# One more first layer by seven products, w1 asked for ahead of w2, and the striking out queued behind the list

## The chip, the core and the metric

The kernel runs on one core of a Trainium2 chip. The core has several engines with a queue of instructions each: TensorE (PE, matrix products; its loads of stationary weights are listed apart, as PEld), VectorE (DVE), ScalarE (ACT), GpSimd (POOL, which here mostly issues gathers and scatters) and SyncE (SP, which issues the plain transfers). A queue is worked off in order; between queues, semaphores make one engine wait for another. The metric is the time of one execution on the device, in microseconds (us). The kernel before takes 395.65 us (median of 3 runs, 395.48 to 396.61).

## The reference

The task joins an attention block to a layer of experts. The attention is a recurrence over 768 steps, for 4 batches of 8 heads of 48 elements:

```python
for t in range(S):
    cur = np.einsum('bhd,bhe->bhde', u[None] * kt, vt)
    y[:, :, t] = np.einsum('bhd,bhde->bhe', rt, state + cur)
    state = w[None, :, :, None] * state + np.einsum('bhd,bhe->bhde', kt, vt)
```

Its output is 3072 rows (tokens) of D = 384. Each row is then given to one of E = 8 experts, and each expert takes exactly 384 rows: all 3072 x 8 scores are sorted downwards, and a score's row goes to the score's expert unless the row has one already or the expert is full. Each expert then does two dense layers on its rows, without bias:

```python
h = np.maximum(x[mask] @ w1[e], 0.0)      # w1[e]: 384 x 1024
out[mask] = h @ w2[e]                     # w2[e]: 1024 x 384
```

Everything is 32-bit floating point.

## The kernel before

**Stages.** The attention fills the first 150 us or so, in an order written out by hand. The remaining 245 us belong to the experts: seven of them in turn with all their 384 rows (numbered 1 to 7 in the order in which the assignment fills them), and one, the "star", in two pieces: 256 rows already within the attention, the last 128 at the very end. In this second part the program text gives the work, and a planner at compile time orders the instructions of each engine by its own cost estimates; on the chip each queue then keeps that order.

**An expert.** `run` (from L1764) goes through the experts. For each it does a first layer (`hid`, 1024 x 384 hidden values, kept transposed) and a second layer. A product of 128 x 128 weights with 128 x 384 data takes TensorE two records in the trace, because the numbers have 32 bits.

- The plain first layer, `hidden` (L1613; its products are line L1621), does 24 products of 128 x 384.
- The other, `hidden_by_seven` (L1562), splits w1, x and the result into 2 x 2 blocks and gets the four result blocks from seven products of sums of blocks in place of eight, a form of Strassen's method. `weight_sums` (L1538) makes four sums of weight blocks (`first_T`, 128 x 512, line L1545), `row_sums` (L1549) five sums of blocks of rows (`first_S`, 128 x 192), both on VectorE. `FIRST` (L1551) names the products P1 to P7, `FIRST_ORDER` their order. In this case the third 128 of D has no partner and is simply added in, so that the layer takes 44 products of 128 x 192, that is 88 records. ScalarE copies P1, P5 and P6 aside, and VectorE adds other products to them (`kept_P`, L1590, 128 x 384). The products appear as `h_ps`, `hb_ps` and `hc_ps` (L1598).
- The second layer of most experts is `seven` for 256 of the rows (L1695, `pa_ps`, `pb_ps`, `pc_ps`; weight and row sums `T`, `S` on L1670) and a plain `result` for the last 128 rows (L1753, `o_ps`, 16 records). For experts 6 and 7 it is `fifteen`, fifteen products of sums for all 384 rows (L1726); its ten weight sums `W` and eleven sums of hidden blocks `H` come from L1670 too.

Which experts take `hidden_by_seven` is written in one line:

```python
FIRST_BY_SEVEN = 3, 6, 7
```

When expert n is in its second layer, `progress` (in `run`) makes the next expert's `weight_sums` and `turn` makes its turned rows `xT` and `row_sums`, if n + 1 is in that list.

**The assignment.** Beside the products, `walk` (class Assignment, L733) finds out which rows the next expert gets. One search is `likely_steps` (L1021). In each of three rounds VectorE marks the scores above 16 candidate thresholds (`ind`), TensorE counts the marks (L945), VectorE prepares the counts (`own`, `cnt`, `wide`), TensorE adds them over all partitions (L956), and VectorE takes the next finer thresholds from the result (`most`, `full`, `dg`, `cand`; in the last round `full_e`, `dge`, ... `acc`). Then TensorE makes running totals (`st_ps`, L1076 and L1077; for the last expert L1379 and L1380), from which VectorE gets `place`. `tokens` (L1392) makes the list of the expert's rows of it: VectorE `lo`, `hi`, `row`, `oh`, `vals`, TensorE `some_ps` (L1409), VectorE `some`, `part`, TensorE `list_ps` (L1427), VectorE `mine`, `tok` (L1433). `leave` (L1003) strikes the taken rows out of the scores: `fe`, `dead` and a masked write to the scores (L1012), then two small updates. The generator `later` (L1918) hands `run` these steps, a few during each expert; the search that runs during expert n's first layer ends ahead of the fetch for expert n + 1.

**Fetching.** `fetch` (L1521) gathers the rows (`xg`, L1515, GpSimd) and calls `load_weights` (L1497), which makes the expert's `number` on VectorE, reads it into a register of SyncE, and asks for both weights, 1536 KB each, in two transfers from SyncE's queue:

```python
for t, src in ((w2, moe_w2), (w1, moe_w1)):
    nc.sync.dma_start(t, src[ds(E - e, 1)].rearrange("o (c p) f -> p (o c) f", p=128))
```

The tiles w1, w2, xg and xT exist twice, for even and odd experts, so a transfer for expert n waits until expert n - 2 has done with that tile, and what stands behind it in SyncE's queue waits as well.

Of the kernel before, what the change touches and what calls it, by code (L numbers as in the profile page):

```python
# [16 lines left out]
ALU = mybir.AluOpType  # L17
# [715 lines left out]
class Assignment:  # L733
# [689 lines left out]
    def numbers(self, part, NC, tok):  # L1423

        nc, pool, Q = self.nc, self.pool, 128 // self.LO
        list_ps = self.ps.tile([128, NC, Q], F32, name="list_ps", tag="few")
        nc.tensor.matmul(list_ps.rearrange("p c q -> p (c q)"), self.alike, part, start=True, stop=True)  # L1427
        mine = pool.tile([128, NC, Q], F32, name="mine")
        nc.vector.scalar_tensor_tensor(out=mine, in0=list_ps, scalar=float(64 * self.NT),
                                       in1=self.quarter.unsqueeze(1).to_broadcast([128, NC, Q]),  # L1430
                                       op0=ALU.add, op1=ALU.mult)
        with nc.allow_low_precision(reason="whole numbers"):
            nc.vector.tensor_reduce(out=tok, in_=mine, axis=AX.X, op=ALU.add)  # L1433

    def in_order(self, tok):

# [13 lines left out]
def rwkv5_eagle_then_base_layer_balanced(  # L1450
# [34 lines left out]
    class Experts:  # L1485
# [13 lines left out]
        def load_weights(self, n, fmax):  # L1499
            number = walk.outs.tile([1, 1], I32, name="number")  # L1500
            nc.vector.tensor_scalar(out=number, in0=fmax[0:1, :], scalar1=1.0, scalar2=float(E),
                                    op0=ALU.max, op1=ALU.min)
            pool = self.turns[n % 2]
            w1, w2 = pool.tile([128, KD, F], F32, name="w1"), pool.tile([128, KF, DX], F32, name="w2")
            e = nc.values_load(number[0:1, 0:1], engines=(mybir.EngineType.SP,), min_val=1, max_val=E,
                               skip_runtime_bounds_check_because="held between 1 and E")
            for t, src in ((w2, moe_w2), (w1, moe_w1)):
                nc.sync.dma_start(t, src[ds(E - e, 1)].rearrange("o (c p) f -> p (o c) f", p=128))
            return w1, w2

# [248 lines left out]
            nc.scalar.copy(o_sb, o_ps)  # L1759
            self.scatter(o_sb, tok[:, c:c + 1], to)  # L1760

        FIRST_BY_SEVEN = 3, 6, 7

        def run(self, ahead, later, rows, pulls={}, xT=None):  # L1764
            xT, lead = xT or self.turn(ahead), True
# [97 lines left out]
    with ExitStack() as whole:  # L1863
# [68 lines left out]
        def later():  # L1932
            yield from search
            walk.bound(ident)
            now = second
            for n in range(2, 5):
                walk.book(now, first=True)
                yield x.fetch(n, now["fmax"], walk.tokens(now["place"]))
                walk.leave(now)
                yield  # L1940
                now = walk.new_outs()
                yield from walk.likely_steps(**now)
            was = now
            walk.book(was)
            walk.leave(was)
            for n in range(5, E):
                rest = n == E - 1
                yield
                if rest:
                    yield  # L1950
                    now = walk.remainder()
                else:
                    now = walk.new_outs()
                    yield from walk.likely_steps(**now)
                walk.book(now, surely=rest)
                walk.choose(was, now)
                yield x.fetch(n, was["fmax"], walk.tokens(was["place"]))
                if not rest:
                    walk.leave(now)
                was = now  # L1960
            yield
            yield
            tc.mark_branch_hint_location("whole")
            have["ok"] = walk.found()
            yield x.fetch(E, walk.star, walk.tokens(walk.star_place, 1))
# [50 lines left out]
```

## Time and profile before

The profiled execution is one run on the chip with the hardware profiler.

| | before |
|---|---|
| median of 3 runs | 395.65 us (395.48 to 396.61) |
| the profiled execution's own time | 395.83 us |
| its span, from first to last record | 394.1 us |
| granted TensorE clock over the span | 0.998 |
| TensorE busy | 381.2 us, 97% of the span |
| VectorE busy | 281.3 us, 71% |
| ScalarE busy | 169.1 us, 43% |
| GpSimd busy | 141.0 us, 36% |
| weight transfers (w1, w2) | 18 of 1536 KB, median 9.0 us from issue to landing |

Busy time by stretch of the experts' part (the stretches begin and end with a layer):

| stretch, us | what TensorE works on | TensorE busy | VectorE busy |
|---|---|---|---|
| 252.3 to 269.3 | expert 4, first layer (plain) | 16.81 | 14.40 |
| 269.3 to 285.4 | expert 4, second layer | 15.79 | 8.70 |
| 285.4 to 302.15 | expert 5, first layer (plain) | 16.75 | 12.84 |
| 302.15 to 317.8 | expert 5, second layer | | 12.90 |
| 317.8 to 332.7 | expert 6, first layer (by seven) | | 10.83 |
| 332.7 to 347.4 | expert 6, second layer (fifteen) | | 14.34 |
| 347.4 to 362.8 | expert 7, first layer (by seven) | 14.81 | 8.83 |

How to read it: busy times are sums over one engine's instructions; engines work beside each other. A line of the timeline gives the start, the duration, the engine, the line of the kernel, the operation, output and inputs with their shapes, and how many instructions of the kind stand in a row; a bracket gives the idle time of the engine ahead of it, and whose work ended that. Idle time of an engine matters only if others wait for it. Ends of products are modelled, so pitches are taken from start to start.

### The profile page before, as it was taken

The page shows a single profiled execution, that of the slowest core. Times are in us where ns is not written, and L with a number is a line of the kernel's source. Part 1 is how long each engine was busy: PE and PEld are TensorE (multiplying, and loading weights), DVE is VectorE, ACT ScalarE, POOL GpSimd, SP SyncE. Part 2 cuts the span into 40 slices and gives each one's busy share as a digit, 9 for nine tenths or more (in the row PEclk, how much of TensorE's full clock was granted, in tenths as well). Part 3 has the DMA queues.
Part 4 walks back from the last instruction along what each step waited for, and adds up shares of the span by engine and source line. Part 5 has one row for each costly group of instructions (what it writes and reads, how often), then busy time and mean ns, then how long its engine had stood idle before and what let it go on. Part 6 is the DMA issues. An engine that isn't in the chain of part 4 may idle for free. (4 is left out here: it accounts for less than half of the span.)

```text
span 394.1 us, 9090 instructions
## 1 busy us (share of the span) xinstructions
PE 381.2 (97%) x3393; PEld 309.5 (79%) x3393; DVE 281.3 (71%) x959; ACT 169.1 (43%) x452; POOL 141.0 (36%) x173
## 2 busy tenths in 40 slices
PE   8999999999999999999999999999999999999993
PEld 7778888888887766677568799558756889989991
DVE  6855777576786778986859949978378976994530
ACT  4997878788883411222222242121222233234130
POOL 7888877656742013032121121202303202070020
PEclk9999999999999999999999999999999999999999
DMA  9999999987592155461470470109209265181010
GB/s 120 160 182 172 197 196 182 171 175 146 113 360 78 58 188 231 145 237 42 119 280 22 132 290 20 41 2 339 83 20 318 97 214 194 38 331 33 2 62 27
DMA packets 95332, 57.30 MB, mean 145 GB/s; under 512 B 77232, under 2 KB 89520, under 8 KB 95280
## 3 DMA queue, kind: packets, MB, share of 16 engines
q1 hardware_dynamic: 91936, 47.21, 47.7%
q0 software_dynamic: 3104, 9.44, 6.9%
q8 instruction: 28, 0.46, 0.5%
q14 instruction: 24, 0.20, 0.2%
q10 hardware_dynamic: 240, 0.00, 0.0%
HBM read 47.20 MB, written 9.44 MB: 144 GB/s over the span
## 5 line engine op out<-in xcount | busy, mean ns | idle before, releaser
L1621 PE MATMUL h_ps<-xT,w 128*128 128x384 f32 (+1 forms) x264 | 72.6, 427 | 0.0
L495 ACT ACTIVATE AT<-ident,dd 128x128 f32<-128x128 f32 x192 | 59.7, 394 | 1.2 <-DVE dd L448 1.1
L1621 PEld LDWEIGHTS h_ps<-xT,w 128*128 128x128 f32 x264 | 42.0, 191 | 19.6 <-issue 2.2
L1515 POOL DMA_INDIRECT xg<-x_rows,tok x22 | 22.2, 1008 | 92.3 <-PE h_ps L1621 23.7
L1747 POOL DMA_INDIRECT out_dram<-o_all,to x16 | 20.8, 1301 | 85.8 <-DVE o_all L1735 22.2
L508 DVE COPY_PREDICATED AT<-mask,g_ps 128x512 f32<-128x512 uint8 x48 | 32.7, 733 | 13.1 <-PE g_ps L504 11.5
L1624 ACT ACTIVATE hid<-h_ps 128x384 f32<-128x384 f32 (+1 forms) x40 | 17.9, 449 | 54.2 <-PE h_ps L1621 50.9
L1753 PE MATMUL o_ps<-w,hid 128*128 128x384 f32 x96 | 32.5, 490 | 0.0
L504 PE MATMUL g_ps<-rT,kT 48*128 48x128 f32 x384 | 27.9, 284 | 1.0 <-ACT x L561 0.6
L436 POOL TENSOR_TENSOR kss<-krs,wk 128x384 f32<-128x384 f32 x24 | 24.3, 1014 | 8.0 <-DVE krs L340 5.2
L504 PEld LDWEIGHTS g_ps<-rT,kT 48*128 48x128 f32 x384 | 23.4, 187 | 4.3 <-ACT AT L495 0.9
L1753 PEld LDWEIGHTS o_ps<-w,hid 128*128 128x128 f32 x96 | 17.7, 190 | 10.6 <-issue 0.5
L542 PE MATMUL y_ps<-AT,vts 128*64 128x128 f32 x384 | 25.7, 276 | 0.0
L443 POOL TENSOR_TENSOR rk<-rk,u_bc 128x384 f32<-128x384 f32 x24 | 24.2, 1009 | 1.9
L442 POOL TENSOR_TENSOR rk<-krs 128x384 f32<-128x384 f32 x24 | 24.5, 1019 | 0.2 <-DVE chunk L650 0.2
L542 PEld LDWEIGHTS y_ps<-AT,vts 128*64 128x64 f32 x384 | 20.6, 137 | 0.9 <-issue 0.3
L477 DVE TENSOR_TENSOR rT<-rT_ps,WR 112x512 f32<-112x512 f32 x23 | 15.8, 686 | 5.1 <-PE rT_ps L458 5.1
L561 ACT COPY x<-y_ps 128x512 f32<-128x512 f32 x24 | 14.1, 588 | 8.6 <-PE y_ps L542 8.6
L448 DVE TENSOR_REDUCE dd<-rk 128x8 f32<-128x384 f32 x24 | 13.1, 546 | 6.3 <-POOL rk L443 6.3
L458 PE MATMUL rT_ps<-ident,krs 128*112 128x128 f32 x96 | 15.5, 283 | 0.5 <-ACT krs L344 0.4
L1695 PE MATMUL pa_ps<-T,S 128*128 128x192 f32 x80 | 15.8, 331 | 0.0
L1726 PE MATMUL p_ps<-W,H 128*128 128x128 f32 x128 | 15.8, 275 | 0.0
(340 smaller groups left out, 831.3 us busy)
## 6 DMA issues: line engine op xcount, KB each, us to landing
w<-in_moe_w_dram SPq DMA_DIRECT2D x18, 1536.0 KB, 9.0
krs<-in_k_dram SPq DMA_DIRECT2D x24, 192.0 KB, 4.5
krs<-in_r_dram SPq DMA_DIRECT2D x24, 192.0 KB, 5.0
vts<-in_v_dram SPq DMA_DIRECT2D x24, 192.0 KB, 5.0
x_rows<-xr SPq DMA_DIRECT2D x24, 192.0 KB, 3.3
xg<-x_rows,tok POOLq DMA_INDIRECT x22, 4.0
out_dram<-o_all,to POOLq DMA_INDIRECT x16, 2.7
out_dram<-o_sb,to POOLq DMA_INDIRECT x5, 2.6
```

What stands on the lines that cost most here:

```text
L436: self.nc.gpsimd.tensor_mul(self.kss[:, n % self.NS].rearrange("p (g h) d -> p g h d", g=2)[:, :, :, 0:D], src, self.wk.rearrange("p (g h) ...
L442: nc.gpsimd.tensor_mul(rk, self.krs[:, n % self.NK, 1, 0:H, 0:D], self.krs[:, n % self.NK, 0, 0:H, 0:D])
L443: nc.gpsimd.tensor_mul(rk, rk, self.u_bc)
L495: nc.scalar.mul(AT[:, z, a, :], self.ident, dd[:, h:h + 1])
L504: nc.tensor.matmul(g_ps[:, z, a, :], kT[rows, a, :], rT[rows, a, :], start=True, stop=True)
L508: nc.vector.copy_predicated(out=AT[:, z], mask=self.mask.unsqueeze(1).to_broadcast([128, HP, T]), data=g_ps[:, z])
L542: nc.tensor.matmul(yv[q * PD:(q + 1) * PD, o // 2, o % 2, :], lhsT, rhs, start=(o // 2, q) not in seen, stop=stop, skip_group_check=True)
L1515: nc.gpsimd.indirect_dma_start(out=xg[:, c, :], out_offset=None, in_=x_dram[0:within, :], in_offset=bass.IndirectOffsetOnAxis(ap=tok[:, c: ...
L1621: nc.tensor.matmul(h_ps[j][:, at], w1[:, f, ts(j, 128)], xT[:, f, at], start=(f == 0), stop=(f == KD - 1))
L1624: nc.scalar.activation(hid[:, j, 0:m], h_ps[j][:, 0:m], AF.Relu)
L1747: nc.gpsimd.indirect_dma_start(out=to, out_offset=bass.IndirectOffsetOnAxis(ap=tok, axis=0), in_=o_sb, in_offset=None)
L1753: nc.tensor.matmul(o_ps, hid[:, j, ts(c, 128)], w2[:, j, :], start=(j == 0), stop=(j == KF - 1))
```

## The change

Three things are changed. Expert 5 joins the list of experts whose first layer goes by seven products of sums; so its four weight sums and five row sums are made during expert 4's second layer. Of every expert's weights, w1 is now asked for first and w2 second (this holds for all nine pairs, also in the part of the program that only runs if the search fails). And in the last part of `later`, for experts 5 and 6 in the loop, the strike-out `walk.leave(now)` is tied, by `tc.issue_after`, to the last instruction of the list (`tok`, remembered as `walk.listed`): it is placed in the queue behind that instruction, and so is the next search, which reads the scores it writes.

```diff
-            nc.vector.tensor_reduce(out=tok, in_=mine, axis=AX.X, op=ALU.add)
+            self.listed = nc.vector.tensor_reduce(out=tok, in_=mine, axis=AX.X, op=ALU.add)
...
-            for t, src in ((w2, moe_w2), (w1, moe_w1)):
+            for t, src in ((w1, moe_w1), (w2, moe_w2)):
                 nc.sync.dma_start(t, src[ds(E - e, 1)].rearrange("o (c p) f -> p (o c) f", p=128))
...
-        FIRST_BY_SEVEN = 3, 6, 7
+        FIRST_BY_SEVEN = 3, 5, 6, 7
...
                 if not rest:
-                    walk.leave(now)
+                    with tc.issue_after(walk.listed.ins):
+                        walk.leave(now)
                 was = now
```

The order of the instructions in the queues follows from these through the planner. In the compiled program TensorE's queue is the same up to the second layer of expert 2. There the search's counts stand one round earlier. In expert 3's first layer the list's two products stand half a wide product later; in expert 4's first layer `some_ps` stands two wide products earlier. Expert 5's first layer begins, with every number a count of 128 x 192 products (two records each): L956, 5, L945, 5, L956, 5, L945, 5, L956, 7, L1076, 13, L1409, 3, L1427. In expert 7's first layer the star's `list_ps` stands one such product earlier. The rest of TensorE's order is the same. On VectorE, the strike-out stands behind `tok` in the searches of experts 4 and 5's layers, and the additions of `kept_P` in expert 5's first layer stand between `cnt` and `wide` (rounds two and three), ahead of `full_e`, and ahead of `some`.

## The prediction

> **What bounds the kernel now.** I read the page's busy shares first, then its clock row, then the TensorE timeline of the experts' part (150 us to the end), then the VectorE timeline beside it, the weight transfers last.
>
> ```profile
> PE 381.2 (97%) x3393; PEld 309.5 (79%) x3393; DVE 281.3 (71%) x959; ACT 169.1 (43%) x452; POOL 141.0 (36%) x173
> PEclk9999999999999999999999999999999999999999
> w<-in_moe_w_dram SPq DMA_DIRECT2D x18, 1536.0 KB, 9.0
> ```
>
> TensorE (PE) is busy for 381.2 of 394.1 us at an even clock (0.998 over the run), so whatever takes time off PE's own row shortens the run, and a cut elsewhere counts only where PE stood still for it. The timeline (columns: start, us, engine, line, operation, out and in, shape, count; in brackets the idle time before it) shows expert 5's first layer, which the change rewrites:
>
> ```profile
> 280.23 5.32 PE L1753 MATMUL o_ps<-w,hid 128*128 128x384 f32 x16
> 285.39 0.22 PE L956 MATMUL counts<-wide,ones_h 128*128 128x128 f16 x1
> 285.45 2.15 PE L1621 MATMUL h_ps<-xT,w 128*128 128x384 f32 x6
> 287.44 0.25 PE L945 MATMUL counts<-prop,ind 128*128 128x64 bf16 x3
> 287.52 1.54 PE L1621 MATMUL h_ps<-xT,w 128*128 128x384 f32 x4
> 288.90 0.22 PE L956 MATMUL counts<-wide,ones_h 128*128 128x128 f16 x1
> ...
> 302.15 1.46 PE L1695 MATMUL pa_ps<-w,hid 128*128 128x192 f32 x8
> 303.45 1.46 PE L1695 MATMUL pc_ps<-w,hid 128*128 128x192 f32 x8
> ```
>
> The reader is to see three things. There is no bracket: PE doesn't wait here. One product is two records, and records follow at a pitch: 285.45 to 302.15 for 48 wide ones, and (303.45 - 302.15) / 8 = 0.1625 us for one 192 columns wide. And the search ahead of expert 6's fetch is woven in: counting matmuls (L956, L945) stand between the products at places written into PE's queue, and VectorE must answer each before PE reaches the next. VectorE's side of one such exchange:
>
> ```profile
> 285.65 0.29 DVE L1044 TENSOR_REDUCE most<-counts 128x16 f32<-128x128 f32 x1 [4.26 <-PE counts L956]
> 286.67 0.55 DVE L933 TENSOR_TENSOR ind<-m,cand 128x384 bf16<-128x384 f32 x1
> 203.51 1.30 DVE L1545 TENSOR_TENSOR first_T<-w 128x512 f32<-128x512 f32 x2 [4.67 <-DMA w<-in_moe_w_dram]
> 329.11 0.69 DVE L1545 TENSOR_TENSOR first_T<-w 128x512 f32<-128x512 f32 x1 [3.19 <-DMA w<-in_moe_w_dram]
> ```
>
> `ind` ends at 287.22 and L945 starts at 287.44, so PE arrives about 0.2 us after it could. The other two lines are the waits for w1, which lands second of its pair.
>
> **The change part by part.** The sum is made against the profiled execution, 395.83 us (span 394.1 and 1.73 around it); it stands 0.18 over the median 395.65, to which I apply the difference.
>
> *Expert 5's products.* It removes 24 products of 384 columns (48 records) and adds 44 of 192 (88 records). The last sixteen wide records of the second layer before it (312.60 to 317.76, expert 5's own) give 5.16 / 16 = 0.3225; another stretch of 22 (197.22 to 204.40) gives 0.3264. At their middle 0.3244: 48 x 0.3244 = 15.57 us against 88 x 0.1625 = 14.30 us. That is -1.27 (with the two pitches -1.2 to -1.4), all of it on PE's row. Rows that exist already agree: experts 3 and 6 by seven products take 220.85 to 235.83 and 317.81 to 332.69, some 14.9 with their interleaved counts, against 16.70 here.
>
> [...]
>
> *The search inside it.* In the changed queue only five narrow products (10 records, 1.63 us) stand between L956 and L945, five between L945 and the next L956, seven between the last L956 and the totals (L1076). Against that:
> - L956 to L945 needs 285.39 to 287.22 plus a hand-over of about 0.07: 1.9 us. Covered are 1.63 + 0.06 for the count itself, so PE waits about 0.2, twice: +0.4.
> - L945 to L956 needs 287.44 to 288.59 (`wide` begins 288.30 and lasts 0.29) and about 0.07, 1.22. The additions of kept products (`kept_P`, 0.55 each, 0.47 in a row) come into VectorE's queue between `cnt` and `wide` in rounds two and three; 1.69 against 1.63 + 0.06: 0.
> - Last L956 (292.40) to L1076 needs `acc` (294.20 + 0.24 = 294.44), 2.1 us, and the addition of P6 before `full_e`, 0.47: 2.57 against 7 x 0.325 = 2.28: +0.25.
> Together +0.65. Lower bound 0: nothing of it shows, since VectorE is busy for only 12.84 of the 16.75 us here. Upper bound: all five additions land in exchanges in full, 5 x 0.55 = 2.75, with the 0.4: +3.15. I take the middle reading because the additions whose place I see lie in covered stretches except one.
>
> *Sums of weights and rows for expert 5.* Four `first_T` (pitch 0.60) and five `first_S` (0.27), 3.75 us of VectorE in expert 4's second layer, where it is busy 8.70 of 15.79 us: hidden. Without that cover they would cost up to 3.75. The first products need raw weights, only the third kind (P5) needs S1 and T1.
>
> *Striking out behind the list.* `fe`, `dead`, the masked write of LG (0.21 + 0.34 + 0.41) leave the place ahead of the list and stand behind `tok`; behind them now wait SEVEN_LATE's first sum S1 and the next search. In expert 5's second layer P5, which needs S1, starts nine narrow products (2.93 us) behind the list's last matmul (L1427). `tok` ends 0.61 behind that (300.53 + 0.17 - 300.09); the strike-out 0.96, the sums S3 and S1 1.30 (0.65 each, 295.06's row) and some 0.18 of hand-over and small operations make 3.05: 0.12 late. Before, P2 and P5 there lay 0.23 over their pitch in the timeline; I take -0.1 (-0.23 to +0.12). In expert 4's first layer the list's first product (L1409) comes two wide products (4 x 0.3244 = 1.30) earlier:
>
> ```profile
> 269.17 0.31 PE L1409 MATMUL some_ps<-vals,row 128*128 128x48 f16 x6 [0.19 <-DVE vals L933]
> 350.51 0.18 PE L1427 MATMUL list_ps<-part,alike 128*128 128x4 f16 x1 [0.59 <-DVE part L1418]
> ```
>
> It waited 0.19 for `vals` before. Ahead of `vals` VectorE is spared `dead`, LG and the next search's `m`, `prop` and `ind` (pitches there 0.25, 0.33, 0.26, 0.27, 0.47: 1.58); as some filled the 0.36 between `upto` and `after`, which depends on it, I count 1.2 and a wait of 0.29: +0.1 (-0.19, the wait goes, to +0.3, if 1.0 is spared). Expert 3's list comes half a product later: -0.05.
>
> *Star's list.* The second line is PE's longest wait for VectorE in this part. Its L1427 now comes one product (0.325) earlier in PE's queue, while VectorE's `part` is moved by -0.1 to +0.3: +0.2, bounds -0.59 (the wait goes) and +0.62 (0.325 + 0.3).
>
> *w1 ahead of w2.* No instruction is added on SP, POOL or the transfer queue: nine pairs change order, each register load as before. SP waits for the place of the first it asks for. For expert 5 the pair was asked at 265.23 and 265.86, w2 came in 266.3 to 271.5 and w1 270.9 to 275.4: one behind the other, so w1 comes about 5 us earlier and w2 as much later. That ends the waits of 4.67 and 3.19 on VectorE, but PE was busy beside both: 0. Late next is w2: expert 6's ten `W` sums begin when w2 lands, and before waited for it 1.47 us at 302.76; they have till the second layer's products of them. In expert 2's second layer, where VectorE no longer stands waiting for w1, the search's counts move one round earlier in PE's queue: 0, bounds -0.3 to +0.3 (half a round's slack of the kind above).
>
> The trace's first-of-pair transfers land 6.8 us or more after their issue. [...]
>
> Sum: -1.27 + 0.65 - 0.1 + 0.1 - 0.05 + 0.2 + 0 + 0 = -0.47. 395.65 - 0.47 = 395.2 us; profiled 395.4, span 393.6.
>
> **The rivals.** *Clean gain.* The exchanges are covered after all (VectorE's own idle times in that stretch, 0.36 to 0.56 ahead of `own` and `full_e` in its timeline, speak for it) and star's wait shrinks by half: -1.27 - 0.3 - 0.1 = -1.7, or -1.27 alone: 393.9 to 394.4. Against it: 10 narrow records are shorter than the 1.9 us chain.
>
> *VectorE takes over (the other side).* In expert 5's first layer the five additions of kept products fall into the search's exchanges, in front of `wide`, `full_e` and `some`, so that PE stands at L956, L1076 and L1409. Price: 5 x 0.55 + 0.4 - 1.27 = +1.9: 397.5. It decides from waits of 1.27 on, and shows as slower from 2.46 on, which is four of the five additions in full and the 0.4. For it: additions wait for PE's own products, thus for the engine that waits for them. Against: expert 3's layer by seven carries the same five beside three interleaved counts in 14.98 us, and there
>
> ```profile
> 232.68 0.55 DVE L1590 TENSOR_TENSOR kept_P<-kept_P,hc_ps 128x384 f32<-128x384 f32 x1 [3.99 <-PE hc_ps L1598]
> ```
>
> VectorE had been idle 3.99 us.
>
> *w2 now too late.* Expert 6's w2 lands where w1 did (302.2 becomes 306.3), so its ten `W` sums (0.60 pitch, 6.0 us) start 4 us later, and the search and list for 7 or a product by `fifteen` wait: one and a half sums' pitch, +0.9, on the forecast: 396.1, within 0.3%.
>
> **How the numbers follow.** 0.3% is 1.19 us, about what a measurement of this kernel can tell from no change: faster is below 394.46, slower above 396.84. Forecast 0.42 (own range 394.5 to 395.9), clean gain 0.30, VectorE takes over 0.18, w2 too late 0.10, of which 0.02 slower. So faster 0.30, within 0.50, slower 0.20. The forecast's lower bounds reach the clean gain's, its upper ones (3.15, 0.62, 0.3) VectorE's; 393.8 to 397.3 leaves out about 0.2, a tenth on each side.
>
> **What would show it.** Right: 88 records at 0.1625 where the 48 stood; 0.1 to 0.3 us in brackets before two L945 and the L1076 of that layer; no `first_T` line with a DMA behind it; about 0.5 before star's L1427. Clean gain: no bracket there. VectorE: brackets of 0.5 or more naming `wide`, `acc` or `vals`. w2: a bracket before a product by `fifteen` naming `W`. The prediction is wrong if the part up to 204 us differs, or if the narrow pitch exceeds 0.17 there.

## The result, and the profile after

The changed kernel takes 397.25 us (median of 10 runs, 396.84 to 397.54), the kernel before 395.66 (10 runs). The ratio is 1.0035, 95% interval 1.0026 to 1.0045: slower by about 1.4 us (0.0035 of 395.66), just past the 0.3% that the forecast counted as the bound to no change. The forecast was 0.47 us faster. The profiled execution's span is 395.5 us against 394.1.

The page of the changed kernel, its busy shares, clock, the group of gathers (out<-in, count, busy us, mean ns of one, idle before) and the weight transfers:

```profile
PE 380.4 (96%) x3433; PEld 314.2 (79%) x3433; DVE 288.2 (73%) x974; ACT 172.3 (44%) x458; POOL 148.3 (37%) x173
PEclk9999999999999999999999999999999999999997
L1515 POOL DMA_INDIRECT xg<-x_rows,tok x22 | 29.4, 1335 | 89.8 <-PE h_ps L1621 39.7
w<-in_moe_w_dram SPq DMA_DIRECT2D x18, 1536.0 KB, 7.0
```

TensorE is busy 0.8 us less (380.4 for 381.2), in a span that is 1.4 us longer: it stands still for some 2.2 us more. The granted clock was 1.00 in both kernels up to 390 us, behind the last product, so the clock is no part of it. The third line is the odd one. The same 22 gathers took 22.2 us of GpSimd before (mean 1008 ns), and take 29.4 now.

Where the time goes is read from the TensorE timeline, by the start of each stage in both kernels:

| stretch | after less before, us |
|---|---|
| up to expert 3's list | 0.02 |
| expert 3's list, in its first layer | +0.26 |
| expert 4's list | +0.17 |
| turning of expert 5's rows, in expert 4's second layer | +0.44 |
| start of expert 5's first layer to product P2 of its second layer | -0.83 |
| from there to the turn | -0.20 |
| turning of expert 6's rows, in expert 5's second layer | +1.48 |
| the star's list | +0.08 |
| sum | +1.42 |

The two turns, from TensorE's timeline of the changed kernel (brackets: idle time and what ended it):

```profile
268.31 0.31 PE L1409 MATMUL some_ps<-vals,row 128*128 128x48 f16 x6 [0.34 <-DVE vals L933]
...
279.78 0.52 PE L1530 MATMUL xT_ps<-ident,xg 128*128 128x128 f32 x3 [0.63 <-DMA xg<-x_rows,tok]
...
286.33 0.87 PE L1598 MATMUL h_ps<-xT,w 128*128 128x192 f32 x4
287.03 1.14 PE L1598 MATMUL hc_ps<-xT,w 128*128 128x192 f32 x6
288.16 0.26 PE L945 MATMUL counts<-prop,ind 128*128 128x64 bf16 x3
...
311.30 0.52 PE L1530 MATMUL xT_ps<-ident,xg 128*128 128x128 f32 x3 [0.78 <-DVE o_all L1685]
...
312.60 0.52 PE L1530 MATMUL xT_ps<-ident,xg 128*128 128x128 f32 x3 [0.45 <-DMA xg<-x_rows,tok]
...
351.69 0.18 PE L1427 MATMUL list_ps<-part,alike 128*128 128x4 f16 x1 [0.76 <-DVE part L1418]
```

The same transposes in the kernel before:

```profile
278.90 0.52 PE L1530 MATMUL xT_ps<-ident,xg 128*128 128x128 f32 x3 [0.31 <-ACT xT L1531]
...
310.18 0.82 PE L1530 MATMUL xT_ps<-ident,xg 128*128 128x128 f32 x6
...
311.24 0.55 PE L1530 MATMUL xT_ps<-ident,xg 128*128 128x128 f32 x3
```

All three L1530 lines of the changed kernel are transposes of gathered rows (`xg`), and two name the gather's transfer. They start 0.14 us after their rows landed (279.64 and 312.46 by the trace's landing signals). The wait that is put down to `o_all` is the second block of the same rows; `o_all` ended at 311.28, but these rows landed at 311.16, again 0.14 ahead of the transposes. So the rows come late, though both lists are ready in time. GpSimd's timeline of the changed kernel shows why:

```profile
270.57 0.99 POOL L1515 DMA_INDIRECT xg<-x_rows,tok  x1 [16.03 <-PE h_ps L1621]
271.86 4.40 POOL L1515 DMA_INDIRECT xg<-x_rows,tok  x1 [0.30 <-issue]
276.57 0.95 POOL L1515 DMA_INDIRECT xg<-x_rows,tok  x1 [0.30 <-issue]
...
303.14 0.99 POOL L1515 DMA_INDIRECT xg<-x_rows,tok  x1 [14.95 <-PE h_ps L1598]
304.44 4.67 POOL L1515 DMA_INDIRECT xg<-x_rows,tok  x1 [0.30 <-issue]
309.41 0.95 POOL L1515 DMA_INDIRECT xg<-x_rows,tok  x1 [0.30 <-issue]
```

The same six gathers in the kernel before:

```profile
272.82 0.99 POOL L1515 DMA_INDIRECT xg<-x_rows,tok  x1 [18.56 <-PE pc_ps L1695]
274.12 1.30 POOL L1515 DMA_INDIRECT xg<-x_rows,tok  x1 [0.30 <-issue]
275.72 0.98 POOL L1515 DMA_INDIRECT xg<-x_rows,tok  x1 [0.30 <-issue]
...
301.47 0.99 POOL L1515 DMA_INDIRECT xg<-x_rows,tok  x1 [14.15 <-issue]
302.77 0.96 POOL L1515 DMA_INDIRECT xg<-x_rows,tok  x1 [0.30 <-issue]
304.04 1.00 POOL L1515 DMA_INDIRECT xg<-x_rows,tok  x1 [0.31 <-issue]
```

In the changed kernel the second of each three gathers stands for 4.40 and 4.67 us; most others take 0.95 to 0.99 us. And this is what VectorE does in the second case:

```profile
303.38 1.29 DVE L1670 TENSOR_TENSOR S<-hid 128x512 f32<-128x512 f32 x2
304.58 0.68 DVE L1545 TENSOR_TENSOR first_T<-w 128x512 f32<-128x512 f32 x1
305.19 0.68 DVE L1670 TENSOR_TENSOR S<-S,hid 128x512 f32<-128x512 f32 x1
305.79 0.68 DVE L1545 TENSOR_TENSOR first_T<-w,first_T 128x512 f32<-128x512 f32 x1
306.39 0.68 DVE L1670 TENSOR_TENSOR S<-hid,S 128x512 f32<-128x512 f32 x1
307.00 0.68 DVE L1545 TENSOR_TENSOR first_T<-w 128x512 f32<-128x512 f32 x1
307.60 0.68 DVE L1545 TENSOR_TENSOR first_T<-w,first_T 128x512 f32<-128x512 f32 x1
308.20 0.34 DVE L1685 TENSOR_TENSOR o_all<-kept_P,pc_ps 128x192 f32<-128x192 f32 x1
```

Eight sums of 128 x 512 without a pause, each with two inputs in SBUF, and then `o_all`, which takes one input from PSUM (the `_ps` tiles, where TensorE's products land; the other tiles here lie in SBUF). The gather ends at 309.11, which is 0.91 us after `o_all` begins: almost exactly the length of an undisturbed gather. At expert 5 it is the same: `o_all` begins at 275.35, the gather ends at 276.26. The gather looks as if it had got through only when the run ended.

A run as long is new at this place. Before, w1 for the next expert landed second, so `first_T` stood behind other work (308.01 for expert 6) and VectorE's queue behind the list was held up by the wait for w2. Now w1 is there when the list is, and hidden sums and weight sums follow each other without a break just when the gathers are issued. But a run by itself isn't enough. The kernel before has a shorter one at the same place, which ends with an `o_all` at 305.94:

```profile
302.76 0.73 DVE L1670 TENSOR_TENSOR W<-w 128x512 f32<-128x512 f32 x1 [1.47 <-DMA w<-in_moe_w_dram]
303.52 0.69 DVE L1670 TENSOR_TENSOR W<-W,w 128x512 f32<-128x512 f32 x1
304.13 0.68 DVE L1670 TENSOR_TENSOR S<-hid 128x512 f32<-128x512 f32 x1
304.74 0.68 DVE L1670 TENSOR_TENSOR W<-W,w 128x512 f32<-128x512 f32 x1
305.34 0.68 DVE L1670 TENSOR_TENSOR S<-S,hid 128x512 f32<-128x512 f32 x1
```

Two gathers were issued into it, at 302.77 and 304.04, and got through in 0.96 and 1.00 us.

### The profile page after: what moved, and what is told of

Its sections match the earlier page's. It is cut to its first block, busy times and chain, and to the rows that moved or that the text cites. A ratio compares the mean times of both kernels' runs of the same rounds, so it can differ in the third digit from the quotient of the medians.

```text
span 395.5 us, 9206 instructions
## 1 busy us (share of the span) xinstructions
PE 380.4 (96%) x3433; PEld 314.2 (79%) x3433; DVE 288.2 (73%) x974; ACT 172.3 (44%) x458; POOL 148.3 (37%) x173
## 5 line engine op out<-in xcount | busy, mean ns | idle before, releaser
L1515 POOL DMA_INDIRECT xg<-x_rows,tok x22 | 29.4, 1335 | 89.8 <-PE h_ps L1621 39.7
L1621 PE MATMUL h_ps<-xT,w 128*128 128x384 f32 (+1 forms) x216 | 56.1, 412 | 0.0
L1621 PEld LDWEIGHTS h_ps<-xT,w 128*128 128x128 f32 x216 | 33.4, 191 | 14.1 <-issue 1.5
L1624 ACT ACTIVATE hid<-h_ps 128x384 f32<-128x384 f32 (+1 forms) x32 | 14.0, 438 | 42.2 <-PE h_ps L1621 40.7
L1753 PE MATMUL o_ps<-w,hid 128*128 128x384 f32 x96 | 32.3, 489 | 0.0
L1753 PEld LDWEIGHTS o_ps<-w,hid 128*128 128x128 f32 x96 | 17.8, 190 | 11.0 <-issue 0.2
L443 POOL TENSOR_TENSOR rk<-rk,u_bc 128x384 f32<-128x384 f32 x24 | 24.2, 1008 | 1.9
L1586 ACT ACTIVATE hid<-kept_P 128x384 f32<-128x384 f32 x24 | 12.6, 523 | 18.0 <-DVE kept_P L1590 17.6
```

The lines of the kernel that those rows point to most:

```text
L443: nc.gpsimd.tensor_mul(rk, rk, self.u_bc)
L1515: nc.gpsimd.indirect_dma_start(out=xg[:, c, :], out_offset=None, in_=x_dram[0:within, :], in_offset=bass.IndirectOffsetOnAxis(ap=tok[:, c: ...
L1621: nc.tensor.matmul(h_ps[j][:, at], w1[:, f, ts(j, 128)], xT[:, f, at], start=(f == 0), stop=(f == KD - 1))
L1753: nc.tensor.matmul(o_ps, hid[:, j, ts(c, 128)], w2[:, j, :], start=(j == 0), stop=(j == KF - 1))
```

## The experiments

Three theories were to be told apart on the late rows. Theory P (two of the expectations call it the port theory): a run of VectorE instructions with two inputs in SBUF holds up GpSimd's gather. Theory D: the weight transfers, in their new order, crowd out the gathers' transfers. Theory V: VectorE simply has too much to do there. The kernels of one series ran on one chip beside the kernel before; that took 395.75 us in the first series, 397.00 in the second and 396.94 in the third, so only ratios are compared across them. The traces of the second and third series stand 0.4 to 1.1 us behind that of the kernel before already ahead of expert 2's second layer, and lose some 0.45 in the star's last piece, every one of them; where stages are compared below, these two differences are left out.

### A tiny instruction between the sums

```diff
-                nc.vector.tensor_tensor(out=t, in0=at[a], in1=at[b], op=op)
+                made = nc.vector.tensor_tensor(out=t, in0=at[a], in1=at[b], op=op)
+                with tc.issue_after(made.ins):
+                    small = self.first.tile([128, 1], F32, name="small")
+                    nc.vector.tensor_reduce(out=small, in_=ident[:, 0:1], axis=AX.X, op=ADD)
                 at[name] = t
             return at
...
         def row_sums(self, xT):
```

> The changed kernel with one tiny VectorE instruction added behind each of the four weight sums of every expert by seven (a reduction of one column of the identity, one input in SBUF, nothing reads its result); TensorE's order is as in the changed kernel. Three theories on the 1.9 us that the changed kernel loses in the turning of rows (0.44 ahead of expert 5, 1.48 ahead of expert 6). Theory P, shared reading: in the changed kernel the second gather of these two experts stands on GpSimd for 4.40 and 4.67 us in place of 0.96 and ends 0.91 us after VectorE's first instruction with an input in PSUM, so a gapless run of VectorE instructions with two inputs in SBUF holds the gather up, and any instruction between them with one input lets it go. Then the two gathers take at most 2.5 us, the waits at the turned rows (0.63, 0.78, 0.45) shrink to 0.3 or less together, and the time falls by 1.2 to 1.7 us to some 395.7 us, though VectorE gets more to do. Theory D, transfers: the rows come late because w2's packets, now second, fill the transfer engines; then nothing changes, 397.2 us and gathers of 4.4 and 4.7 us. Theory V, VectorE has too much to do there: the time grows by up to 0.3 us, 397.3 to 397.5.

Measured: 395.21 us, ratio 0.9985 (0.9975 to 0.9996). VectorE has more to do, and by the ratios the kernel is faster than the changed one by 2.0 us, and a little faster than the kernel before. GpSimd's second gathers now take 2.60 and 2.28 us, and VectorE's timeline shows where they got through:

```profile
273.00 0.69 DVE L1673 TENSOR_TENSOR S<-hid,S 128x512 f32<-128x512 f32 x1
273.60 0.15 DVE L1548 TENSOR_REDUCE small<-ident 128x1 f32<-128x1 f32 x1
273.67 0.68 DVE L1545 TENSOR_TENSOR first_T<-w,first_T 128x512 f32<-128x512 f32 x1
...
304.43 0.69 DVE L1673 TENSOR_TENSOR S<-S,hid 128x512 f32<-128x512 f32 x1
305.03 0.15 DVE L1548 TENSOR_REDUCE small<-ident 128x1 f32<-128x1 f32 x1
```

The gathers began at 271.93 and 303.69, and so ended at 274.53 and 305.97: 0.93 and 0.94 after the start of the tiny instruction that is shown for each. No bracket at a transpose is left in TensorE's timeline between 265 and 335 us; the turns, compared with the kernel before, gain 0.36 and lose 0.27. At the second, rows are still waited for: those of the third gather landed at 310.50 and were used at 310.63. Theories D and V fall as the main cause in the changed kernel: the order of the transfers is the same, and VectorE's work grew. The landings speak against D too: in the changed kernel the rows that came late ahead of expert 6 landed 2.05 and 2.10 us after their gathers had left GpSimd, as in the kernel before at 275.42 and 276.70 (2.03 and 2.06).

### The same with two inputs

```diff
-                    nc.vector.tensor_reduce(out=small, in_=ident[:, 0:1], axis=AX.X, op=ADD)
+                    nc.vector.tensor_tensor(out=small, in0=ident[:, 0:1], in1=ident[:, 1:2], op=ADD)
```

> The counterpart of the run before: the same tiny instruction in the same places, but with two inputs in SBUF (one column of the identity added to another) in place of one. Theory P, if it is the two inputs that hold the gather and not the lack of a pause: gathers of 4.4 to 5.1 us as in the changed kernel, 397.2 to 397.6 us. If a pause or any short instruction is enough: as the run before, some 395.7 us. Theory D and theory V: as they expect of the run before, 397.2 to 397.5 us; so D and V are told from P by the pair and not by this run.

Measured: 395.25 us, ratio 0.9984 (0.9973 to 0.9995), the second gathers 2.60 and 2.28 us. The strict form of P is wrong: a tiny instruction with two inputs lets the gather through just as well. What held it in the changed kernel is not any single instruction with two inputs, but a run of them (4.40 and 4.67 us).

### A measured dose of both kinds

In the kernel before, thirteen instructions each behind the lists of experts 3 and 4, in a stretch where VectorE otherwise has pauses; nothing reads their results. The trace calls their input `LG`.

```diff
+                if n > 2:
+                    with tc.issue_after(walk.listed.ins):
+                        for i in range(13):
+                            big = x.first.tile([128, walk.NT, E], F32, name=f"big{i % 2}")
+                            if n == 3:
+                                nc.vector.tensor_tensor(out=big, in0=walk.ML, in1=walk.ML, op=ADD)
+                            else:
+                                nc.vector.tensor_reduce(out=big[:, :, 0], in_=walk.ML, axis=AX.X, op=ADD)
                 yield ahead
                 walk.leave(now)
```

> The kernel before with thirteen more VectorE instructions behind the list of expert 3 (the scores added to themselves, 128 x 192, two inputs in SBUF, pitch near 0.27, 3.5 us in all; nothing reads the result) and thirteen behind the list of expert 4 (the greatest in place: a sum over the same scores, one input, about the same pitch). VectorE stands idle at both places before (4.67 and 3.99 us), and the gathers take 0.95 to 0.99 us there. If a run of instructions with two inputs holds a gather: at expert 3 one gather takes up to 3.5 us, at expert 4 none over 1.1. If any dense run does: both. If only long instructions do (128 x 512, as in the changed kernel): neither. The time by itself says nothing; PE is not meant to wait: 395 to 396.5 us.

Measured in one run: 397.24 us beside 397.00. VectorE's timeline at the two lists, expert 3's (198 us) and expert 4's (228 us):

```profile
198.13 2.76 DVE L1944 TENSOR_TENSOR big<-LG 128x192 f32<-128x192 f32 x10
200.82 0.68 DVE L1670 TENSOR_TENSOR S<-hid 128x512 f32<-128x512 f32 x1
201.42 0.42 DVE L1012 COPY_PREDICATED_SCALAR LG<-dead,neg 128x192 f32 x1
...
228.30 2.68 DVE L1946 TENSOR_REDUCE big<-LG 128x24 f32<-128x192 f32 x10
```

And GpSimd's timeline of the same kernel, the gathers beside them:

```profile
199.32 3.02 POOL L1515 DMA_INDIRECT xg<-x_rows,tok  x1 [0.30 <-issue]
...
229.41 0.96 POOL L1515 DMA_INDIRECT xg<-x_rows,tok  x1 [0.30 <-issue]
230.67 0.95 POOL L1515 DMA_INDIRECT xg<-x_rows,tok  x1 [0.30 <-issue]
```

This speaks for P in its corrected form. Ten reductions with one input, dense for 2.68 us, don't touch the gather (0.96, 0.95 us). Ten additions with two inputs at the same pitch, and the sum S behind them, hold it for 3.02 us: it ends at 202.34, 0.92 after the sum gave way to the masked write of LG at 201.42. So density alone doesn't hold a gather, and instructions of 128 x 512 aren't needed: here an unbroken run of ten additions of 128 x 192 and one sum, with two inputs in SBUF, did it. This is one profile, and the two kinds differ in operation and output too (128 x 192 written against 128 x 24), so it isn't shown that it is the second input, and not one of these, that counts.

By what means such a run holds the gather, no run here shows. The traces give the lengths alone: 3.02 us beside the two-input run of the dose against 0.96 beside its one-input run, and 4.67 us in the changed kernel, over seven instructions in a row.

### The parts alone and in pairs

Each is the kernel before with the named parts of the change.

```diff
-        FIRST_BY_SEVEN = 3, 6, 7
+        FIRST_BY_SEVEN = 3, 5, 6, 7
```

> The kernel before with nothing but expert 5 among those by seven. The layer itself gained 0.83 us in the changed kernel (1.27 less 0.44 of waits in the search's exchanges). Theory P: expert 5's gathers are as before, since its weight sums come behind them in the queue; at expert 6 the run ahead of the first sum from PSUM is four to five instructions with two inputs, 2.4 to 3 us, so one gather takes 2 to 3.5 us and the turn loses 0 to 0.6: 394.8 to 395.5 us. Theory D: transfers are in the order of before, no turn loses: 394.8 us. Theory V: 3.75 us more of VectorE in expert 4's second layer and less slack behind: both turns lose as in the changed kernel, 396.7 us.

Measured: 395.73 us, ratio 1.0003 (0.9994 to 1.0013). The layer and the stretch behind it give 0.84, no turn loses, as P and D expect; but 0.76 is lost at a place that no theory named, in expert 6's first layer:

```profile
331.20 0.92 PE L1598 MATMUL h_ps<-xT,w 128*128 128x192 f32 x4 [0.49 <-DVE kept_P L1590]
```

The addition `kept_P` is late on VectorE. In this kernel w1 for expert 7 is the second of its pair; VectorE stands 4.45 us for it until the first `first_T` starts at 329.53, and the additions stand behind in the same queue (330.14 and 330.60). So expert 5 by seven by itself is worth nothing here: what it gives is taken one layer later.

```diff
-            for t, src in ((w2, moe_w2), (w1, moe_w1)):
+            for t, src in ((w1, moe_w1), (w2, moe_w2)):
```

> The kernel before with nothing but w1 asked for ahead of w2. VectorE's queue behind the list for expert 6 is then seven instructions with two inputs in SBUF without a break (the weight sums for expert 6 and the sums of hidden blocks), about 4.2 us from the landing of w1 near 302.2 us on. Theory P: expert 6's second or third gather is held till about 307 us (4 us in place of 1.0) unless it comes in just ahead of the run, and the turn ahead of expert 6 loses up to 1.1 us; with the 0.26 that the changed kernel lost at expert 3's list (its counts moved by the same part) 395.9 to 397.0 us. Expert 5's turn is as before (0.3 wait). Theory D: w2 lands late for experts 5 and 6 alike, so both turns lose, 1.9 us: 397.5 us. Theory V: 395.7 us, for VectorE gets nothing new to do.

Measured: 396.48 us, ratio 1.0015 (1.0003 to 1.0027), with runs between 395.54 and 397.02. Its profile is of its slowest run. There nothing is gained or lost at expert 6's turn (its gathers take 0.99, 0.97 and 1.49 us; one got through within a run, so here too a run doesn't hold every gather), 0.28 is lost at expert 3's list and 0.25 gained at the turn of expert 5's rows. The rest of its 1.2 us of longer span lies behind the last product: on the chain that ends last, the last but one scatter landed in 4.64 us in place of 2.82, and the final one went out at 389.39 in place of 388.19 though the last product ended 0.07 later than before.

```diff
-            nc.vector.tensor_reduce(out=tok, in_=mine, axis=AX.X, op=ALU.add)
+            self.listed = nc.vector.tensor_reduce(out=tok, in_=mine, axis=AX.X, op=ALU.add)
...
-                    walk.leave(now)
+                    with tc.issue_after(walk.listed.ins):
+                        walk.leave(now)
```

> The kernel before with nothing but the strike-out and the next search queued behind the list. Up to expert 4's list TensorE's order is that of before; there the list comes earlier, which cost 0.36 in opened and best5 and was given back at the next turn of rows (0.36 less wait for them). Behind both lists small instructions stand among VectorE's long ones, so no gather is held for over 1.5 us. Time as before within 0.3 us; if the strike-out by itself delays the second layer's sums (prediction: by 0.12) 0.1 to 0.4 us more.

Measured: 396.93 us, ratio 1.0003 (0.9989 to 1.0016): nothing, as expected. Expert 4's list costs 0.15, against 0.17 in the changed kernel, the turn of expert 5's rows gives back 0.36, and the stretch from there to expert 6's turn some 0.3 more. But a gather was held for 2.26 us behind expert 5's list, against the expectation of 1.5: a sum, `prop` (128 x 192) and a sum stand without a pause there too. No wait came of it, since the list came earlier.

> Expert 5 by seven and the strike-out behind the list, but w2 first as before. Expert 5's layer gives 0.84; then w1 for expert 7 lands second of its pair, VectorE stands waiting for it with an addition of a kept product (L1590) behind it, and TensorE waits in expert 6's first layer, as in five_alone (0.76 lost at 331.2 us, 0.49 of it in one bracket). So as five_alone: the time of before within 0.3 us. If the strike-out is what cures expert 6's layer, 0.8 us less than before.

Measured: 397.79 us, ratio 1.0026 (1.0017 to 1.0036): slower than expected. Its profile is of its fastest run (396.43) and shows what was expected (0.57 lost in expert 6's first layer, with a bracket of 0.30 that names `kept_P`); why nine of ten runs take some 1.3 us more it doesn't show. That stays open.

> w1 ahead of w2 and the strike-out behind the list, expert 5's first layer plain as before. The run of seven long instructions with two inputs stands behind expert 6's list, so its second gather is held for 2 to 4.5 us if the port theory holds; the rows are then just in time for a layer that is 1.27 us longer ahead of it: 0 to 0.5 us lost at that turn, and 0.28 at expert 3's list. 0.3 to 0.8 us over before. The transfer of w1 for expert 7 starts late, as in the changed kernel, so rows aren't crowded out by it.

Measured: 396.94 us, ratio 1.0002 (0.9991 to 1.0014), a little better than expected: 0.28 is lost at expert 3's list and 0.15 at expert 4's, and 0.37 comes back at the turn of expert 5's rows, 0.3 behind it. Its gathers for expert 6 take 0.99, 0.97 and 1.49 us.

> The kernel before with expert 5 by seven and w1 ahead of w2, but the strike-out where it was. Behind expert 6's list VectorE's queue is the same run of eight instructions of 128 x 512 as in the changed kernel (sums of hidden blocks and weight sums in turn); behind expert 5's list small instructions stand between the four weight sums. If the long run holds the gather: expert 6's second gather takes over 4 us, the turn ahead of expert 6 loses some 1.5 us, the turn ahead of expert 5 nothing: 395.7 - 0.84 + 0.27 + 1.5 = 396.6 us. If the strike-out behind the list is what makes the rows late: no gather over 1.5 us, 395.1 us. If w2's transfer does: both turns lose, 397.0 us.

Measured: 400.13 us, ratio 1.0074 (1.0057 to 1.0091), the slowest of all, and not for the reason that P gives. Its profile is of the slowest of its four runs (401.14). The gathers got through (1.27, 0.96 and 0.94 us) beside a run of seven such sums, and still the turn ahead of expert 6 loses 4.1 us. GpSimd's timeline of this kernel, the second and third gather for expert 6:

```profile
305.75 0.96 POOL L1515 DMA_INDIRECT xg<-x_rows,tok  x1 [0.30 <-issue]
307.01 0.94 POOL L1515 DMA_INDIRECT xg<-x_rows,tok  x1 [0.30 <-issue]
```

TensorE's timeline, at the last transposes of those rows:

```profile
314.65 0.87 PE L1530 MATMUL xT_ps<-ident,xg 128*128 128x128 f32 x3 [1.79 <-DMA xg<-x_rows,tok]
315.32 2.13 PE L1695 MATMUL pa_ps<-T,hid 128*128 128x192 f32 x6
```

And the busy share of the transfer engines between 300 and 320 us, a digit for each half us (9 is busy throughout):

```profile
DMA  8999999999999999999999999991000000000007
```

Here theory D fits. The last gather left GpSimd at 307.95, its rows landed at 314.52 and were used at 314.65, when the transfer engines had just been busy without a gap till 313.5: SyncE had asked for w1 of expert 7 at 304.14, in the midst of the gathers, because w1's place comes free after the first layer and the expert's number was ready. In the changed kernel that request goes out at 312.04, since the number hangs on the strike-out, which stands behind the list there. The kernel with w1 alone asks as early (302.56) and its transfer engines are busy without a gap till 311 us, but without expert 5 by seven its gathers begin 2.5 us sooner (301.69 for 304.17), and its rows are there in time. So the third part of the change keeps a third weight transfer out of the gathers' way. At this turn the pair loses 4.08 (0.94 of it by the low clock below) and the changed kernel 1.48, and in the whole the ratios differ by 0.0039, some 1.5 us; that is nowhere in the prediction. No run changed the transfers by themselves, so their part rests on these records. TensorE also ran at a granted clock of 0.58 between 315 and 318 us, after it had stood still for half of the five us before (1.00 till 310): six records took 2.13 us that take 1.14 in the other kernels at this place.

### Versions meant to be faster

This asks for w1 first from expert 5 on alone, on top of the kernel with the tiny one-input instruction:

```diff
-            for t, src in ((w1, moe_w1), (w2, moe_w2)):
+            for t, src in ((w1, moe_w1), (w2, moe_w2)) if n >= 5 else ((w2, moe_w2), (w1, moe_w1)):
```

> The changed kernel with the tiny one-input instruction behind each weight sum (as in opened) and w1 ahead of w2 from expert 5 on alone; experts 1 to 4 ask in the order of before. In opened the layer of expert 5 gave 0.84, the turn ahead of expert 5 another 0.36, and what stayed lost was 0.27 at expert 3's list, 0.36 at expert 4's list (the strike-out's part) and 0.14 at the star's list. If 0.27 belongs to w1's place for experts 2 to 4, as the unchanged TensorE order up to expert 4's list in this kernel suggests: 0.27 less than opened, 394.95 us. If it is only how the runs fall: 395.2.

Measured: 396.25 us beside 397.00, ratio 0.9980 (0.9970 to 0.9989). Expert 3's list loses nothing now (0.00 in place of 0.26), which puts that loss down to w1's place for the early experts; but 0.14 is lost in expert 2's second layer, where tiny instructions stand between expert 3's weight sums, and no run parts the two. By the ratios it beats both kernels (the changed one stands at 1.0035); from the kernel with the tiny instruction alone (0.9985) it can't be told apart.

Expert 4 by seven too, on top of the last:

```diff
-        FIRST_BY_SEVEN = 3, 5, 6, 7
+        FIRST_BY_SEVEN = 3, 4, 5, 6, 7
```

> As best5, with expert 4's first layer by seven products too. By the terms measured at expert 5 (1.27 of products less 0.44 of waits in the search's exchanges) 0.83 less than best5: 394.1 us. If theory V holds after all (two more layers' sums in VectorE's queue are too much: 3.75 us of sums in expert 3's second layer, where VectorE is busy 15.4 of 16.5 us) PE waits for the search or for the sums there by 1 to 3 us and the time is 395.1 to 397 us. The gathers for expert 5 stand behind the sums only as far as the tiny instructions let them.

Measured: 399.40 us, ratio 1.0066 (1.0047 to 1.0086). Expert 4's layer gives about 0.9, but its list comes late (the first gather at 274.76 in place of 271.12 in best5), and TensorE stands 2.62 us at the turn for the rows. The three gathers take 0.99, 1.13 and 0.95 us; here it is the search that makes the rows late: `vals`, behind additions and sums on VectorE, starts at 270.79 where it starts at 268.35 in best5.

A tiny instruction between the hidden sums as well, at expert 5, on top of best5 (`last` is the sum just made, and `self.now` the expert's number):

```diff
+                if name in ("S1", "S2") and self.now == 5:
+                    with tc.issue_after(last.ins):
+                        nc.vector.tensor_reduce(out=self.first.tile([128, 1], F32, name="small"), in_=ident[:, 0:1],
+                                                axis=AX.X, op=ADD)
```

> As best5, with one more tiny one-input instruction behind each of the sums S1 and S2 of expert 5's second layer. In best5 expert 6's second gather still took 2.27 us and let go at the first tiny instruction, four long ones after the run's begin; now one stands 1.2 us earlier. Port theory: that gather takes 1.0 to 1.3 us, and the 0.15 us that the turn ahead of expert 6 still lost goes: 0.1 to 0.2 us less than best5, a ratio to before of 0.9975. If the rows come late for their transfers: as best5, 0.998.

Measured: 396.07 us beside 396.94, ratio 0.9979 (0.9970 to 0.9988). The gather does as P says, 1.06 us in place of 2.27, but the time hardly follows: the turn still loses 0.13, against 0.15 in best5. What is left there is 0.27 us ahead of the weight load of the last transposes. The profile puts it down to ScalarE's copy of rows (L1531), but the rows of the third gather landed at 311.20, 0.13 ahead of these transposes, so it is the rows again. They weren't held on GpSimd: that gather left it at 306.81 after 0.95 us, and landed 4.39 us later, where 2.05 and 2.10 were seen in the changed kernel. Of its 16 landing signals 15 were in by 309.65 and the last came 1.55 us after them. So at this small remainder theory D fits, as the second branch of the expectation has it; why one signal comes so late is open.

## Why the prediction was wrong, point by point

- *Expert 5's products*: -1.27 was forecast, and with *the search inside it* at +0.65 the layer should have given 0.62. It gave 0.83, so the exchanges cost 0.44, most of it in the places that were named. The ten narrow records ahead of the first L945 (286.33 to 288.16 in the first fence of TensorE) take 1.83 where ten pitches are 1.63, those ahead of the second 1.87 (290.02 to 291.89), and both places had been 0.04 over their pitches before: 0.16 and 0.20. The chain of L956 to L945, put at 1.9, measured 1.89 and 1.92. The third place, ahead of the totals, cost 0.1 and not 0.25. The mechanism was right, the term too large by 0.2; part of that is that the waits were counted against bare pitches, which the layer before hadn't kept either.
- *Sums of weights and rows for expert 5: hidden.* This is the step that failed, together with the next. It asked whether VectorE had time, and VectorE had. It didn't ask who else is kept waiting while VectorE runs without a pause. The sums stand exactly where the gathers are issued, and with the hidden sums they hold the second gather for 4.40 us at expert 5, where an undisturbed one takes 0.97: +0.44 at the turn, costed at nothing. The strike-out has a share in it: by itself it holds that gather for 2.26 us (iss_alone).
- *w1 ahead of w2: 0.* "That ends the waits of 4.67 and 3.19 on VectorE, but PE was busy beside both" is true and beside the point, and so is "No instruction is added on SP, POOL or the transfer queue": the gathers on POOL stayed 22, but two of them stood. With w1 early, eight sums follow each other behind expert 6's list, the second gather stands 4.67 us, and the turn loses 1.48, costed at nothing. No one part does that: with one part or two, no gather for expert 6 took over 1.49 us, so in these runs it took all three to set the long run against this gather, and the price can't be shared out among them. "Late next is w2" was wrong: no bracket of TensorE names `W`, and VectorE begins these sums at 308.62 without a wait. And in expert 3's first layer the list lost 0.26, where -0.05 was forecast, which best5 puts down to this part.
- *Striking out behind the list.* Expert 4's list: +0.1 forecast, +0.17 measured (bracket 0.34 where 0.29 was expected). Expert 5's second layer: -0.1 forecast, -0.20 measured. The part that matters was missed: it makes expert 7's number late and so keeps w1 of expert 7 away from the gathers (five_w1 against the changed kernel, some 1.5 us; by the records, not by a run of its own).
- *Star's list*: +0.2 forecast, +0.08 measured; the bracket is 0.76 in place of 0.59, but it comes a product earlier.
- *Landings of the weights*: for the first of a pair 6.8 us or more was read; it landed 6.8 to 8.1 us after its issue in the kernel before, and 6.3 to 7.0 us in the changed one. No term rested on it.
- The sum: -0.47 forecast, +1.42 by the trace. The terms that were named came to -0.50, with errors of up to 0.3 that cancel; the two turns that were not named add 1.92, which is the whole miss and the change of sign.
- *The rivals.* The forecast for the slower side, VectorE in the search's exchanges, was priced at 397.5 and the time was 397.25, but by luck, since the mechanism was another: its brackets of 0.5 naming `wide` or `acc` are not there. The clean gain came nearest in opened, where the two turns together no longer lose, at 395.21; the lists of experts 3 and 4 and the exchanges keep the rest of it.

## What to carry to other kernels

When work is moved or hurried on VectorE, look not only at who waits for it, but at what GpSimd has to issue beside it: an unbroken run of VectorE instructions with two inputs in SBUF kept a gather standing here to its end (4.40 and 4.67 us in place of 0.97), and one tiny instruction inside the run, which costs 0.07 us of VectorE, let it through each time. Look also at what a stall keeps apart: VectorE's wait of 1.47 us for w2 (302.76) is gone in the changed kernel, and eight sums stand there in a row, with the gather of 4.67 us beside them. And where rows and weights are moved at the same time, what makes a weight request late can be worth more than what makes it early: some 1.5 us here, by the records of five_w1 and the changed kernel.

## What the runs showed of the hardware

- A gather of 128 rows took GpSimd 0.94 to 0.99 us in most cases. Beside an unbroken run of VectorE instructions with two SBUF inputs it took 4.40 and 4.67 us (128 x 512) and 3.02 us (128 x 192), and ended 0.91 to 0.94 us after the run did. In a run as dense with one input: 0.96 and 0.95 us.
- A 128 x 1 instruction of either kind ended the hold (opened and closed: second gathers of 2.60 and 2.28 us in place of 4.40 and 4.67). A boundary between two long ones sometimes did (304.26 for 1.49 us in w1_alone, 305.75 for 0.96 us in five_w1) and mostly not (six boundaries in a row in the changed kernel). In the kernel before, two gathers issued into a run took 0.96 and 1.00 us (302.77, 304.04). What decides is open.
- The kernel before has a transfer that stands as long: a scatter of 4.36 us at 346.55, in a stretch of sums for expert 6; no wait of TensorE follows from it.
- The end of the kernel hung on the landing of its last but one scatter: 2.82 us in the kernel before, 4.64 us in the slowest run of w1_alone, whose span was 1.2 us longer with its last product 0.07 later.
- The landing of a gather hung on one of its 16 signals: in five_w1 15 were in by 313.02 and the last came at 314.52, in best5t by 309.65 and 311.20.
- After TensorE had stood still for about half of 5 us, its granted clock was 0.58 over the next 3 us (five_w1); after the 1.2 us of the changed kernel's wait it stayed at 1.00. In best45 six records behind a stand of 2.62 us took 0.98 us from start to start (281.69 to 282.67), the usual time, so no rule follows from the one case.
- A product of 32-bit numbers stands in the trace as two records, one of 16-bit numbers as one: in the kernel before 96 records of L1753 for 48 products, 63 of L945 for 63. The transposes of 32-bit rows (L1530) are one each, 66 for 66.
